# A third group of the first layer by seven products in its second matmul, and the second layer's first operands formed on GpSimd and read back from HBM

## The chip, the cores and the metric

One core of a Trainium2 chip runs the whole program. The metric is the time of one execution in device microseconds (us); the median of three runs is given for the kernel before. The engines are named as in the profile: PE (TensorE matmul), PEld (its weight load), DVE (VectorE), ACT (ScalarE), POOL (GpSimd) and SP (SyncE, which here only issues DMAs).

## What is computed

```python
x = attention(q, k, v, omega)                 # (4 batches, 8 heads, 576, 64) -> 2304 tokens x 512
x = square(maximum(x @ moe_w_in, 0)) @ moe_w_out        # first layer,  512 -> 2048 -> 512
h = x @ moe2_w_in                                       # second layer, 512 -> 2048 -> 512
g = where(h > 0, h, exp(minimum(h, 0)) - 1)
return g @ moe2_w_out                                   # float32, 2304 x 512
```

The attention is a linear one (random features, no softmax over tokens). All is float32. The change lies in the two layers alone.

## The kernel before

**Precision.** A float32 operand goes through PE as two limbs: a high one, cast on ACT to a rounded float32, and a low one, the rest, made on DVE by `minus` (L77). A product of two operands is three matmuls (high by high, high by low, low by high).

**Tiling.** Tokens come in four blocks of 512 (i = 0 to 3) and a left-over block B of 256. The hidden width of each layer is cut into four groups g of 512. A *tour* is one block in one group of one layer, written here (layer, group, block), so (0,3,1) is block 1 in the first layer's last group. Blocks go in the order 0, B, 1, 2, 3. The first group of the first layer is written apart; from (0,1,0) on a tour is one turn of the loop in `toured`.

**One tour.** The first product (`times`, L759) follows Strassen's scheme in Winograd's form: seven products of 12 matmuls (256 columns each) in the order b, t3, t2, p, t1, t4, q, named by the operand that is read; t1 to t4 are differences of quarters of x. In block B there are no seven products but four sets of 12. Behind the products stand additions on DVE (c22 at L1061, c21 at L1066), the activation on ACT, and the splitting into limbs. The second product of a tour runs between the first products of the *next* tour: `earlier(0)` to `earlier(3)` run four parts of it. In a group that is listed in `SECOND` these parts are again Winograd's seven products (`quadrants`, calling `strassen`, L836), 84 matmuls for a full block: p1 and p5, then p6 and p2, then p7 and p3, then p4. Their inputs are the four quarters of the activation (11, 12, 21, 22) and four differences t1 to t4 of them, made by `difference` (L924) and split by `halved` (L930, limbs at L77). In any other group of the first layer they are four calls of `chunk` (L818) of 24 matmuls, 96 in all, whose inputs are the four quarters alone. The left-over block has 48 either way. The sums of the outputs go into pages `ya` on DVE: `grown` (L910) for Strassen, `summed` (L942) for `chunk`.

**Chores.** Every tour also makes weights for a group to come: tiles are loaded by SP, an ACT and two DVE passes bring them into order (`cm` L135, `cv` L143 and L150), then they are cast (ACT, L189, `wh`) and their low limbs made (DVE, L77, `wl`). Where a weight's quarters are to be combined (all of w_in, and w_out of the groups in `SECOND`), each odd tile takes four more DVE operations of 128x256 (L171 to L174 for w_out, L176 to L179 for w_in). The chores are spread over the *slots* of the tour: `slot` stands four times in a full tour (between the products) and twice in block B.

**The second layer's operands.** When block i of the first layer's last group is done, `operands1` forms t1 to t4 from its four `ya` pages by `terms` on DVE at once (block B: one difference d), and puts seven splits (block B: three) into the list `later`. Each `slot` takes three of them: a cast on ACT (L621) and a `minus` on DVE. The limbs are written to HBM (`keep`, by SP) for the groups 1 to 3 of the second layer, which read them five products ahead (`read`, `XA = 5`). For group 0 of the second layer the limbs stay in SBUF: `split` enters them in `x_t`, and `read` skips that group.

**Order.** No scheduler moves anything: each engine executes in the order in which the program is written. An engine that waits holds up all that is written behind it on that engine.

## Time and profile before

| | |
|---|---|
| median of three runs | 911.29 us (911.05 to 911.65) |
| the profiled execution, its time | 911.45 us |
| its span in the trace | 909.7 us (1.75 us lie around it) |
| PE busy | 898.5 us, 99% |
| DVE busy | 682.3 us, 75% |
| ACT busy | 591.9 us, 65% |
| POOL busy | 86.7 us, 10%, all in the first 140 us |
| granted TensorE clock | full in all 40 slices of the span (the 2.4 GHz level) |

The first layer's group 2 (Strassen in both products) runs from 343.35 us, the start of tour (0,2,B), to 435.29 us, the start of (0,3,B), counted by its second products: 91.94 us. Group 3 (`chunk`) runs from there to 532.31 us: 97.02 us. Group 1 (Strassen) took 91.99 us, from 251.36 to 343.35. Tour starts that the text needs: (0,1,3) 302.32, (0,2,0) 322.98, (0,2,B) 343.35, (0,2,1) 360.07, (0,2,2) 375.65, (0,2,3) 395.54, (0,3,0) 415.42, (0,3,B) 435.29, (0,3,1) 452.29, (0,3,2) 468.47, (0,3,3) 489.74, (1,0,0) 511.05 us. Since PE is all but never idle, what matters in this profile is not a busy share but the few places where a PE row carries a bracket with an idle time, and the length of each tour against the number of its matmuls.

### The profile page before, as it was taken

Reading aid. Unit: us, or ns where it says so; the run is one execution under the profiler, and the core shown is the slowest. Engines: PE = TensorE matmul, PEld = TensorE weight load, DVE = VectorE, ACT = ScalarE, POOL = GpSimd, SP = SyncE. Lnnn points to the kernel's source line nnn. Section 1 sums busy time; section 2 is a strip of 40 time slices with the busy share of each in tenths; the row PEclk is TensorE's granted clock in tenths of the full one; section 3 lists DMA queues with packets and bytes.
Section 4 is the critical chain, followed back from the end, with each engine's and each line's share of the span. In section 5 each row is a group of like instructions: output and inputs, shape, how many; then the busy total and the mean of one; then the engine's idle time right before and its main releaser. Section 6 shows DMA issues by size and latency. Waiting matters only on the chain.

```text
span 909.7 us, 20185 instructions
## 1 busy us (share of the span) xinstructions
PE 898.5 (99%) x7637; PEld 839.5 (92%) x7637; DVE 682.3 (75%) x1254; ACT 591.9 (65%) x1260; POOL 86.7 (10%) x188
## 2 busy tenths in 40 slices
PE   8999999999999999999999999999999999999997
PEld 7888999998999999999999999899899889989986
DVE  5898874688786888777879897966597649766553
ACT  7999877664767675766266666755476638654551
POOL 4678730000000000000000000000000000000000
PEclk9999999999999999999999999999999999999999
DMA  9576522525998676577589654276458655662551
GB/s 249 160 196 159 170 83 80 172 93 173 330 375 300 210 253 236 178 234 254 192 290 333 237 207 162 93 255 203 166 196 272 226 165 191 231 206 92 214 179 70
DMA packets 132096, 183.84 MB, mean 202 GB/s; under 512 B 33952, under 2 KB 65696, under 8 KB 132000
## 3 DMA queue, kind: packets, MB, share of 16 engines
q1 hardware_dynamic: 131152, 182.14, 60.3%
q8 instruction: 60, 0.98, 0.4%
q10 hardware_dynamic: 848, 0.43, 0.2%
q14 instruction: 36, 0.29, 0.1%
HBM read 145.29 MB, written 37.22 MB: 201 GB/s over the span
## 4 chain that ended last, share of the span: by engine, by line
PE 88%; DVE 4%; ACT 4%; DMA 2%; issue 1%; SPq 0%; POOL 0%; DVEq 0%; ACTq 0%; POOLq 0%
PE py L810 22%; PE pb L759 13%; PE pa L759 8%; PE pw L759 8%; PE py L818 5%; PE ph L549 5%; PE py L585 5%; PE pb L836 4%; PE px L836 3%; PE po L759 2%; PE pe L759 2%; PE pr L836 2%; PE pn L437 1%; PE px L469 1%; DMA xsph<-xd00p 1%
## 5 line engine op out<-in xcount | busy, mean ns | idle before, releaser
L782 DVE SCALAR_TENSOR_TENSOR r<-r,t 128x512 f32<-128x512 f32 x72 | 49.5, 687 | 90.2 <-ACT t L781 90.2
L810 PE MATMUL py<-wh,gh 128*128 128x512 f32 x288 | 113.6, 395 | 0.0
L810 PE MATMUL py<-wl,gh 128*128 128x512 f32 x288 | 113.6, 394 | 0.0
L810 PE MATMUL py<-wh,gl 128*128 128x512 f32 x288 | 113.6, 394 | 0.0
L77 DVE TENSOR_TENSOR gl<-gf,gh 128x512 fp32r<-128x512 f32 (+1 forms) x122 | 77.3, 634 | 8.7 <-ACT gh L792 5.1
L810 PEld LDWEIGHTS py<-wh,gl 128*128 128x128 f32 x288 | 54.2, 188 | 12.7
L810 PEld LDWEIGHTS py<-wl,gh 128*128 128x128 f32 x288 | 54.2, 188 | 10.0
L810 PEld LDWEIGHTS py<-wh,gh 128*128 128x128 f32 x288 | 54.2, 188 | 9.9
L792 ACT CAST gh<-gf 128x512 fp32r<-128x512 f32 x72 | 44.4, 616 | 25.7 <-DVE gf L783 24.8
L942 DVE TENSOR_TENSOR ya<-py,ya 128x512 f32<-128x512 f32 x72 | 46.5, 683 | 7.0 <-PE py L810 6.1
L780 ACT ACTIVATE r<-gf 128x512 f32<-128x512 f32 x72 | 45.6, 633 | 2.3
L1047 ACT COPY pb<-pa 128x512 f32<-128x512 f32 x28 | 16.1, 574 | 46.1 <-PE pa L759 46.1
L135 ACT ACTIVATE cm<-st 128x512 f32<-128x512 f32 x64 | 44.3, 700 | 2.0 <-DMA st<-in_moe_w_out_dram 1.7
L1055 ACT COPY us<-pb 128x512 f32<-128x512 f32 x28 | 16.4, 586 | 43.4 <-PE pb L759 35.0
L781 ACT ACTIVATE t<-gf 128x512 f32<-128x512 f32 x72 | 44.3, 616 | 0.0
L150 DVE SCALAR_TENSOR_TENSOR cv<-cm,cv 128x512 uint32<-128x512 uint32 x64 | 43.3, 685 | 0.8
L1061 DVE TENSOR_TENSOR c<-pb,vs 128x512 f32<-128x512 f32 x28 | 19.3, 690 | 29.2 <-PE pb L759 23.4
L818 PE MATMUL py<-gh,wh 128*128 128x256 f32 x144 | 40.5, 282 | 0.0
L818 PE MATMUL py<-gh,wl 128*128 128x256 f32 x144 | 40.5, 281 | 0.0
L818 PE MATMUL py<-gl,wh 128*128 128x256 f32 x144 | 40.5, 281 | 0.0
L549 PE MATMUL ph<-xh,wh 128*128 128x256 f32 (+1 forms) x128 | 38.8, 303 | 0.0
L585 PE MATMUL py<-gh,wh 128*128 128x256 f32 (+1 forms) x128 | 38.5, 301 | 0.0
(1128 smaller groups left out, 3318.3 us busy)
## 6 DMA issues: line engine op xcount, KB each, us to landing
st<-in_moe_w_in_dram SPq DMA_DIRECT2D x32, 512.0 KB, 5.3
st<-in_moe_w_out_dram SPq DMA_DIRECT2D x32, 512.0 KB, 3.6
vk<-in_v_dram SPq DMA_DIRECT2D x32, 128.0 KB, 4.7
out_dram<-ya SPq DMA_DIRECT2D x16, 256.0 KB, 2.4
ld0k<-in_k_dram SPq DMA_DIRECT2D x4, 256.0 KB, 4.4
ld0q<-in_q_dram SPq DMA_DIRECT2D x4, 256.0 KB, 5.0
ld1k<-in_k_dram SPq DMA_DIRECT2D x4, 256.0 KB, 5.3
ld1q<-in_q_dram SPq DMA_DIRECT2D x4, 256.0 KB, 4.6
```

Of the source, the lines that this page charges most:

```text
L77: eng.tensor_tensor(out=out, in0=whole, in1=hi.bitcast(F32), op=ALU.subtract)
L135: nc.scalar.activation(out=staged[p][1], in_=staged[p][0][:, :, 1].bitcast(F32), func=AF.Prelu, scale=REBIAS, alpha=NEGATIVE)
L549: nc.tensor.matmul(ph[:, :n], wt[:, cs], x_part(xt, i, c)[:, n0:n1], start=(m == 0), stop=(m == 3 * KD - 1))
L585: nc.tensor.matmul(y, w[:, ts], a, start=j == 0 and m == 0 and t % per == 0, stop=j == GF - 1 and m == 2, skip_group_check=per > 1,)
L759: nc.tensor.matmul(y[:, pr * HN:(pr + 1) * HN], wt[:, ws], xs[v][:, e * HN:(e + 1) * HN], start=fresh and first and pr == 0 and m == 0, st ...
L780: nc.scalar.activation(out=r, in_=gf, func=AF.Exp, scale=-1.0)
L782: nc.vector.scalar_tensor_tensor(out=r, in0=r, scalar=1.0, in1=t, op0=ALU.add, op1=ALU.mult)
L792: nc.scalar.copy(out=gh, in_=gf)
L810: nc.tensor.matmul(y_t[l, u], a[:, s0], w, start=first and pr == 0 and m == 0, stop=last and pr == 1 and m == 2,)
L818: nc.tensor.matmul(y_t[l, u][:, e * HN:(e + 1) * HN], w[:, ts], a[:, pr * HN:(pr + 1) * HN], start=first and pr == 0 and m == 0 and e == 0 ...
L836: nc.tensor.matmul(y[:, e * HN:(e + 1) * HN], w[:, cs], a[:, pr * HN:(pr + 1) * HN], start=fresh and pr == 0 and e == 0 and m == 0, stop=p ...
L942: nc.vector.tensor_tensor(out=ya_t[key], in0=y_t[l, u], in1=ya_t[key], op=ALU.add)
```

## The change

Three things change, and with them the rows of the engines.

- `SECOND` gains (0,3): the first layer's last group makes its second product by seven products. Its w_out tiles then need the extra combinations.
- The second layer's operands: the four differences (block B: one) are formed by GpSimd instead of DVE, as entries of `later` among the splits, in the order b, t3 formed, t3, t1 and t2 formed, t2, p, t1, t4 formed, t4, q. Their limbs stay no longer in SBUF for group 0 of the second layer; that group reads them from HBM like the others, 31 pairs of 512 KB.
- The pace of `later` in the tours of the first layer's last group: two entries of a slot while block 0's or B's entries stand first, otherwise one, where it was three. Elsewhere it stays three.

```diff
-    SECOND = ((0,1),(0,2))
+    SECOND = ((0,1),(0,2),(0,3))
...
         kept.append(lambda: keep(moe, i, name, ((h,), (l,))))
-        if moe:
-            x_t[1, 0, i, name] = h, l
...
-    def terms(moe, i, b):
-
-        tt = nc.vector.tensor_tensor
...
-        tt(out=ts["t1"], in0=b[1, 0], in1=b[0, 0], op=ALU.subtract)
-        tt(out=ts["t2"], in0=b[1, 1], in1=ts["t1"], op=ALU.subtract)
-        tt(out=ts["t3"], in0=b[1, 1], in1=b[1, 0], op=ALU.subtract)
-        tt(out=ts["t4"], in0=b[0, 1], in1=ts["t2"], op=ALU.subtract)
...
-        made = [(name, b[l, k]) for name, l, k in PARTS[i == B]] + found
-        later.extend(lambda name=name, t=t: split(1, i, name, t) for name, t in made)
...
+            nc.gpsimd.tensor_tensor(out=ts[name], in0=ts.get(a, a) if isinstance(a, str) else a, in1=ts[c] if isinstance(c, str) else c, op=ALU.subtract)
...
+        made("b", (0, 0))
+        formed(("t3", (1, 1), (1, 0)))
+        made("t3")
+        formed(("t1", (1, 0), (0, 0)), ("t2", (1, 1), "t1"))
+        made("t2")
+        made("p", (0, 1))
+        made("t1")
+        formed(("t4", (0, 1), "t2"))
+        made("t4")
+        made("q", (1, 1))
...
-            if reads[n_read[0]][0][:2] != (1, 0):
-                load_x(*reads[n_read[0]])
+            load_x(*reads[n_read[0]])
...
-    def slot(chores, left):
+    def slot(tour, chores, left):
 
         run(kept)
         run(chores, -(-len(chores) // left))
-        run(later, 3)
+        n = 3 if tour[0] or tour[1] < NG - 1 else 2 if owed and owed[0] in (0, B) else 1
+        run(later, n)
+        del owed[:n]
```

In the order that the builds give, tile names carry layer, group and block, and a running number; L numbers are those of each kernel's own file (after: `strassen` L848, `grown` L922, `difference` L936, c22 L1075, c21 L1080).

DVE around the third slot of tour (0,2,2), where `cv0_12_1` and `cv0_13_1` are two w_out tiles of group 3 and `ya0` sums of the tour before. The kernel before:

```order
L910 TENSOR_TENSOR ya0_1_0_0_3525<-pr0_2_1_6494,ya0_1_0_0_3525 128x512
L910 TENSOR_TENSOR ya0_1_0_1_3527<-pr0_2_1_6494,ya0_1_0_1_3527 128x512
L910 TENSOR_TENSOR ya0_1_256_0_3711<-px0_2_1_6480,ya0_1_256_0_3711 128x512
L150 SCALAR_TENSOR_TENSOR cv0_12_1_6474<-cm0_12_1_6472,cv0_12_1_6474 128x512
L150 SCALAR_TENSOR_TENSOR cv0_13_1_6553<-cm0_13_1_6478,cv0_13_1_6553 128x512
L77 TENSOR_TENSOR gl22_0_2_2_6664<-g22_0_2_2_6630,gh22_0_2_2_6663 128x512
L910 TENSOR_TENSOR ya0_1_0_1_3527<-pb1_4651,ya0_1_0_1_3527 128x512
L910 TENSOR_TENSOR ya0_1_0_0_3525<-pb2_4653,ya0_1_0_0_3525 128x512
```

The kernel after:

```order
L922 TENSOR_TENSOR ya0_1_0_0_3525<-pr0_2_1_6494,ya0_1_0_0_3525 128x512
L922 TENSOR_TENSOR ya0_1_0_1_3527<-pr0_2_1_6494,ya0_1_0_1_3527 128x512
L922 TENSOR_TENSOR ya0_1_256_0_3711<-px0_2_1_6480,ya0_1_256_0_3711 128x512
L150 SCALAR_TENSOR_TENSOR cv0_12_1_6474<-cm0_12_1_6472,cv0_12_1_6474 128x512
L150 SCALAR_TENSOR_TENSOR cv0_13_1_6553<-cm0_13_1_6478,cv0_13_1_6553 128x512
L171 TENSOR_TENSOR cs0_13_1_6635<-cv0_13_1_6553 128x256
L172 TENSOR_TENSOR cv0_13_1_6553<-cv0_12_1_6474,cv0_13_1_6553 128x256
L173 TENSOR_TENSOR cs0_13_1_6635<-cv0_13_1_6553 128x256
L174 TENSOR_TENSOR cd0_13_1_6636<-cv0_12_1_6474,cs0_13_1_6635 128x256
L77 TENSOR_TENSOR gl22_0_2_2_6670<-g22_0_2_2_6630,gh22_0_2_2_6669 128x512
L922 TENSOR_TENSOR ya0_1_0_1_3527<-pb1_4651,ya0_1_0_1_3527 128x512
L922 TENSOR_TENSOR ya0_1_0_0_3525<-pb2_4653,ya0_1_0_0_3525 128x512
```

The four combinations of 128x256 now stand between the second L150 and `gl22`, the low limb of the quarter 22, as they do in group 1's tours for the tiles of group 2. The same stands in tour (0,2,3) for the tiles 14 and 15.

DVE from tour (0,3,1) into (0,3,2); `wl1_0b`, `cv1_3_0` and the four combinations are chores for the second layer, `gl` and `glt` are low limbs of this tour's activation. The kernel before:

```order
L77 TENSOR_TENSOR gl21_0_3_1_7759<-gf21_0_3_1_7730,gh21_0_3_1_7731 128x512
L77 TENSOR_TENSOR wl1_0b_7764<-cv1_1_0_7324,wh1_0b_7627 128x512
L150 SCALAR_TENSOR_TENSOR cv1_3_0_7696<-cm1_3_0_7629,cv1_3_0_7696 128x512
L176 TENSOR_TENSOR cs1_3_0_7767<-cv1_2_0_7537,cv1_3_0_7696 128x256
L177 TENSOR_TENSOR cv1_3_0_7696<-cv1_3_0_7696 128x256
L178 TENSOR_TENSOR cs1_3_0_7767<-cv1_3_0_7696,cv1_2_0_7537 128x256
L179 TENSOR_TENSOR cd1_1_0_7454<-cv1_2_0_7537,cs1_3_0_7767 128x256
L77 TENSOR_TENSOR wl1_0c_7772<-cs1_1_0_7453,wh1_0c_7631 128x512
L942 TENSOR_TENSOR ya0_4_0_0_4559<-py0_3_4_0_0_7553,ya0_4_0_0_4559 128x512
L942 TENSOR_TENSOR ya0_4_0_1_4561<-py0_3_4_0_1_7554,ya0_4_0_1_4561 128x512
L636 TENSOR_TENSOR d1_4_7776<-ya0_4_0_1_4561,ya0_4_0_0_4559 128x512
L77 TENSOR_TENSOR gl12_0_3_1_7818<-gf12_0_3_1_7754,gh12_0_3_1_7755 128x512
```

The kernel after:

```order
L936 TENSOR_TENSOR gt1_0_3_1_7750<-g11_0_3_1_7628,gt1_0_3_1_7750 128x512
L77 TENSOR_TENSOR wl1_0b_7761<-cv1_1_0_7347,wh1_0b_7634 128x512
L150 SCALAR_TENSOR_TENSOR cv1_3_0_7687<-cm1_3_0_7636,cv1_3_0_7687 128x512
L176 TENSOR_TENSOR cs1_3_0_7764<-cv1_2_0_7560,cv1_3_0_7687 128x256
L177 TENSOR_TENSOR cv1_3_0_7687<-cv1_3_0_7687 128x256
L178 TENSOR_TENSOR cs1_3_0_7764<-cv1_3_0_7687,cv1_2_0_7560 128x256
L179 TENSOR_TENSOR cd1_1_0_7496<-cv1_2_0_7560,cs1_3_0_7764 128x256
L77 TENSOR_TENSOR wl1_0c_7769<-cs1_1_0_7495,wh1_0c_7638 128x512
L77 TENSOR_TENSOR pl1_0_7772<-ya0_0_0_1_2970,ph1_0_7771 128x512
L77 TENSOR_TENSOR t1l1_0_7776<-t1_1_0_7644,t1h1_0_7775 128x512
L77 TENSOR_TENSOR glt2_0_3_1_7820<-gt1_0_3_1_7750,ght2_0_3_1_7819 128x512
L77 TENSOR_TENSOR gl12_0_3_1_7824<-g12_0_3_1_7746,gh12_0_3_1_7823 128x512
```

The two sums and the term of block B (`ya0_4`, `d1_4`) have gone from here; two low limbs of block 0's operands (`pl1_0`, `t1l1_0`) stand now ahead of `glt2` and `gl12`.

ACT in tour (0,3,1): `wh1_0b`, `cm1_3_0` and `wh1_0c` are chores, L621 the casts of block 0's operands, and the rows behind them the activation of the quarter 22. The kernel before:

```order
L189 CAST wh1_0b_7627<-cv1_1_0_7324 128x512
L135 ACTIVATE cm1_3_0_7629<-st1_3_0_7326 128x512
L189 CAST wh1_0c_7631<-cs1_1_0_7453 128x512
L621 CAST t3h1_0_7633<-t3_1_0_7489 128x512
L621 CAST t2h1_0_7637<-t2_1_0_7488 128x512
L621 CAST t1h1_0_7641<-t1_1_0_7487 128x512
L773 ACTIVATE r22_0_3_1_7681<-c220_3_1_7500 128x512
L774 ACTIVATE gh22_0_3_1_7683<-r22_0_3_1_7681 128x512
```

The kernel after:

```order
L189 CAST wh1_0b_7634<-cv1_1_0_7347 128x512
L135 ACTIVATE cm1_3_0_7636<-st1_3_0_7349 128x512
L189 CAST wh1_0c_7638<-cs1_1_0_7495 128x512
L621 CAST t3h1_0_7640<-t3_1_0_7568 128x512
L930 ACTIVATE g22_0_3_1_7681<-c220_3_1_7523 128x512
L931 ACTIVATE g22_0_3_1_7681<-g22_0_3_1_7681 128x512
L621 CAST t2h1_0_7694<-t2_1_0_7692 128x512
L930 ACTIVATE g21_0_3_1_7723<-c210_3_1_7522 128x512
```

One cast of an operand, that of t3, now stands ahead of the activation of 22 where three stood; the casts of t2 and t1 have moved behind it. In all, PE has 48 matmuls fewer, ACT 46 instructions more (1260 before), DVE 14 more (1254 before), POOL 17 more (128x512 each), and SP issues 62 reads of 256 KB more.

## Rows read from the trace of the kernel before

**Rows 1.** Page, part 1: busy us, share of the span, instructions.

```profile
PE 898.5 (99%) x7637; PEld 839.5 (92%) x7637; DVE 682.3 (75%) x1254; ACT 591.9 (65%) x1260; POOL 86.7 (10%) x188
```

**Rows 2.** Windows, one a tour; last five: us, engines busy (x), PEclk, DMA, GB/s.

```profile
302.32:322.98 20.66, 20.43 (x170) 20.03 (x169) 17.62 (x31) 14.04 (x27) 0.00 (x0) 1.00 0.78 254
322.98:343.35 20.37, 20.13 (x170) 19.93 (x169) 17.16 (x31) 14.73 (x27) 0.00 (x0) 1.00 0.70 234
343.35:360.07 16.72, 15.92 (x134) 15.72 (x133) 13.03 (x23) 9.44 (x18) 0.00 (x0) 1.00 0.70 236
360.07:375.65 15.58, 15.58 (x135) 15.58 (x134) 10.77 (x20) 8.54 (x15) 0.00 (x0) 1.00 0.57 187
...
395.54:415.42 19.88, 19.88 (x171) 19.88 (x169) 16.09 (x29) 13.99 (x26) 0.00 (x0) 1.00 0.83 280
415.42:435.29 19.87, 19.87 (x171) 19.87 (x169) 15.41 (x27) 12.94 (x25) 0.00 (x0) 1.00 0.68 217
452.29:468.47 16.18, 15.86 (x134) 15.65 (x133) 10.39 (x18) 9.75 (x18) 0.00 (x0) 1.00 0.66 227
489.74:511.05 21.31, 21.31 (x182) 21.31 (x181) 19.78 (x34) 12.34 (x22) 0.00 (x0) 1.00 0.84 299
```

**Rows 3.** Waits of PE, 234 to 640 us: releaser, idle us, count, largest.

```profile
PE px L836 <- DVE wl_10B L77: 0.8, 1, 0.8
...
PE pb L759 <- DVE c L1061: 0.3, 1, 0.3
```

**Rows 4.** Timeline of PE: start us, us, operation [idle before <-releaser].

```profile
307.43 0.39 PE L836 MATMUL pr<-glt,wh_4B 128*128 128x256 f32 x1 [0.23 <-DVE glt L77]
...
332.16 0.39 PE L836 MATMUL pb<-glt,wh_4C 128*128 128x256 f32 x1 [0.24 <-DVE glt L77]
...
347.99 0.39 PE L836 MATMUL px<-gh,wl_10B 128*128 128x256 f32 x1 [0.80 <-DVE wl_10B L77]
...
384.41 0.28 PE L836 MATMUL pb<-glt,wh_8C 128*128 128x256 f32 x1
...
466.95 0.39 PE L759 MATMUL pb<-xsqh,wh_12d 128*128 128x256 f32 x1 [0.32 <-DVE c L1061]
```

**Rows 5.** Timeline of DVE and ACT, tours (0,1,2) and (0,2,1).

```profile
301.79 0.42 DVE L171 TENSOR_TENSOR cs<-cv 128x256 f32<-128x256 f32 x1
...
370.26 0.69 DVE L1061 TENSOR_TENSOR c<-pb,vs 128x512 f32<-128x512 f32 x1 [2.61 <-PE pb L759]
...
371.03 0.60 ACT L189 CAST wh_12c<-cs 128x512 fp32r<-128x512 f32 x1
...
371.60 0.69 DVE L1066 TENSOR_TENSOR c<-pw,us 128x512 f32<-128x512 f32 x1 [0.65 <-PE pw L759]
...
374.56 0.69 DVE L77 TENSOR_TENSOR gl<-g,gh 128x512 fp32r<-128x512 f32 x1 [0.73 <-ACT gh L930]
...
377.65 0.69 DVE L77 TENSOR_TENSOR glt<-gt,ght 128x512 fp32r<-128x512 f32 x1 [0.48 <-ACT ght L930]
...
382.64 0.68 DVE L77 TENSOR_TENSOR glt<-gt,ght 128x512 fp32r<-128x512 f32 x1
```

**Rows 6.** Timeline of POOL and DVE in the attention stage.

```profile
118.48 1.04 POOL L321 TENSOR_TENSOR s23q<-ld3q 128x512 f32<-128x512 f32 x1
...
118.93 0.88 DVE L77 TENSOR_TENSOR gl<-gf,gh 128x256 fp32r<-128x256 f32 x1
...
113.28 0.44 DVE L77 TENSOR_TENSOR gl<-gf,gh 128x256 fp32r<-128x256 f32 x1
```

**Rows 7.** Windows: the stage from c22 of (0,3,1) on, and two stretches of DMA.

```profile
466.21:577.55 111.34, 111.02 (x846) 106.58 (x845) 98.82 (x170) 73.11 (x131) 0.00 (x0) 1.00 0.64 228
...
250.00:285.00 35.00, 35.00 (x297) 34.87 (x296) 26.03 (x45) 23.58 (x43) 0.00 (x0) 1.00 1.02 379
...
505.00:590.00 85.00, 85.00 (x600) 79.45 (x598) 75.61 (x128) 57.85 (x104) 0.00 (x0) 1.00 0.49 171
```

**Rows 8.** DMA issues: count, KB each, us to landing.

```profile
xst2h<-xd10t SPq DMA_DIRECT2D x3, 256.0 KB, 4.2
```

More of the change, by code (lines that the diff above doesn't have):

```diff
@@ L526, in linear_attention_two_ffn_kernel @@
     later, kept, unhurried, sums, carried, seeds = [], [], [], [], [], []
-    wholes = {}
+    wholes, owed = {}, []
     behind = [[], []]
@@ L629, in prepare @@
         run(later, n)
-    def terms(moe, i, b):
-        tt = nc.vector.tensor_tensor
-        if i == B:
-            d = page([W], f"d{moe}_{i}")
-            tt(out=d, in0=b[0, 1], in1=b[0, 0], op=ALU.subtract)
-            return [("d", d)]
-        ts = {name: page([W], f"{name}_{moe}_{i}") for name in TS}
-        tt(out=ts["t1"], in0=b[1, 0], in1=b[0, 0], op=ALU.subtract)
-        tt(out=ts["t2"], in0=b[1, 1], in1=ts["t1"], op=ALU.subtract)
-        tt(out=ts["t3"], in0=b[1, 1], in1=b[1, 0], op=ALU.subtract)
-        tt(out=ts["t4"], in0=b[0, 1], in1=ts["t2"], op=ALU.subtract)
-        return [(name, ts[name]) for name in ("t3", "t2", "t1", "t4")]
     PARTS = {False: (("b", 0, 0), ("p", 0, 1), ("q", 1, 1)), True: (("u", 0, 0), ("v", 0, 1))}
@@ L649, in operands1, with term, made, formed @@
         b = {(l, k): ya_t.pop((i, l, k)) for l in range(1 if i == B else 2) for k in range(2)}
-        found = terms(1, i, b)
-        made = [(name, b[l, k]) for name, l, k in PARTS[i == B]] + found
-        later.extend(lambda name=name, t=t: split(1, i, name, t) for name, t in made)
+        ts = {}
+        def term(name, a, c):
+            ts[name] = page([W], f"{name}_1_{i}")
+            a, c = (t if isinstance(t, str) else b[t] for t in (a, c))
+            nc.gpsimd.tensor_tensor(out=ts[name], in0=ts.get(a, a) if isinstance(a, str) else a, in1=ts[c] if isinstance(c, str) else c, op=ALU.subtract)
+        def made(name, key=None):
+            later.append(lambda: split(1, i, name, b[key] if key else ts[name]))
+            owed.append(i)
+        def formed(*terms_):
+            for t in terms_:
+                later.append(lambda t=t: term(*t))
+                owed.append(i)
+        if i == B:
+            made("u", (0, 0))
+            made("v", (0, 1))
+            formed(("d", (0, 1), (0, 0)))
+            made("d")
+            return
+        made("b", (0, 0))
[8 more added lines that the diff above has]
+        made("q", (1, 1))
     def piece0(d, i, l, k):
@@ L1004, in toured @@
                 chores = chores_of(tour)
-                slot(chores, 2)
+                slot(tour, chores, 2)
                 earlier(0)
@@ L1027, in toured @@
                     act_b(tour, "21")
-                slot(chores, 1)
+                slot(tour, chores, 1)
                 earlier(3)
@@ L1050, in toured @@
             chores = chores_of(tour)
-            slot(chores, 4)
+            slot(tour, chores, 4)
             earlier(0)
@@ L1057, in toured @@
             act(tour, "11", a)
-            slot(chores, 3)
+            slot(tour, chores, 3)
             earlier(1)
@@ L1068, in toured @@
             act(tour, "22", c22)
-            slot(chores, 2)
+            slot(tour, chores, 2)
             earlier(2)
@@ L1085, in toured @@
                 act_b(tour, "21")
-            slot(chores, 1)
+            slot(tour, chores, 1)
             earlier(3)
```

## The prediction

> **What bounds the kernel now.** I read the page first: PE is busy for 898.5 of 909.7 us, DVE for 682.3 [rows 1]. So a matmul less is time gained, as long as nobody makes PE wait instead. The second view is the length of each tour against its matmuls, by windows. A tour with 84 + 84 matmuls takes 19.88 us, so 0.1183 us for one; a tour of the last group with 84 + 96 takes 21.31 us, 0.1184 us for one [rows 2]. PE is at the 2.4 GHz level in every window (PEclk 1.00), so these lengths can be compared. The third view is PE's waits between 234 and 640 us: only a few, each below 1 us, and those of interest are on DVE [rows 3]. The fourth is the timeline around them. There one must not stop at the bracket: the tour from 302.32 us has 0.23 us in a bracket before `pr` [rows 4], yet it is 0.78 us longer than the tour from 395.54 us with the same matmuls [rows 2]; the matmul behind the wait is itself long (0.39 us). So I price a wait by the tour's length, not by its bracket. The last view is DVE's load where the change acts, from c22 of (0,3,1) on: 98.82 of 111.34 us, 170 instructions [rows 7]. That is the point of this case: PE gives up work there, and DVE gets more.
>
> **The change part by part.** All sums start from the profiled execution, 911.45 us (span 909.7 us and 1.75 us around it); the median of the three runs is 0.16 us lower.
>
> *Matmuls.* In four tours 96 become 84: 48 x 0.1184 = 5.7 us less. The block B tour keeps its 48.
>
> *One wait that goes.* The tour from 452.29 us is 16.18 us long; its 84 + 48 = 132 matmuls are worth 15.6 [rows 2]. PE waits there for c22 on DVE [rows 3, 4]. By the order of ACT three casts of operands stand before that point now, and one afterwards. I take the whole 0.6 us off.
>
> *Combinations of group 3's w_out.* Eight more DVE operations of 128x256, 0.42 us each [rows 5], come into tours (0,2,2) and (0,2,3), and three low limbs into the tours up to (0,3,B). The eight stand at the same places as in group 1's tours, whose order the changed tours repeat row by row. So I copy those lengths: the tour from 302.32 us takes 20.66 and that from 322.98 us 20.37, against 19.88 and 19.87 for group 2's without the combinations [rows 2]: 0.8 + 0.5 us. What is late there is `glt`, which PE needs for p5 and p6 [rows 4].
>
> *Block B of group 3.* With Strassen, (0,3,B) begins its second products with `w_out` combinations, as (0,2,B) does; there PE waits for `wl_10B` [rows 3, 4] and the tour takes 16.72 us, against 15.58 us for the same 132 matmuls in the next one [rows 2]. The new tour needs `wl_14B` at the same place: 1.1 us.
>
> *DVE and ACT between (0,3,1) and (0,3,2).* The nearest rows are those of (0,2,1), with the same products and no operands of the second layer. There c22 starts at 370.26 us, as soon as PE has its product (2.61 us of idle DVE before it) [rows 5]. In the changed kernel the cast of t3 stands behind the cast `wh..c` on ACT, which ends at 371.03 + 0.60 = 371.63 us [rows 5], and its low limb stands ahead of c22 on DVE: 371.63 + 0.60 + 0.69 = 372.92, so c22 is 2.7 us late. Behind it are three more low limbs (t2, p, t1) ahead of `glt2`: 3 x 0.69 = 2.1 us. Against these 4.8 us stand three idle gaps of DVE, 0.65 + 0.73 + 0.48 = 1.9 us, and the time from the end of the low limb `glt` (382.64 + 0.68 = 383.32 us) to the matmul that reads it (384.41 us), 1.1 us [rows 4, 5]. So PE waits 4.8 - 1.9 - 1.1 = 1.8 us at p6. The ends: nothing, if PE's own earlier delays make room, and 4.8 us.
>
> *The rest of the stage.* By the order DVE has seven operations more in the stage from 466.21 to 577.55 us (the three or four differences and sums of each Strassen tour, less the 17 terms). At 98.82 / 170 = 0.58 us each [rows 7] that is 4.1 us: 102.9 us in 111.34 - 5.7 + 2.1 = 107.8 us. DVE keeps 4.9 us of idle time, so it isn't the bound on the whole, only at places. For such a place in (0,3,3), where DVE is already busy for 19.78 us [rows 2] and the tour shrinks to about 19.9, I add 0.3 us (between none and 1). ACT, 73.11 us in this stage [rows 7], takes the 40 further instructions beside PE.
>
> *Terms on GpSimd.* An operation of 128x512 takes POOL 1.04 us. While it runs, a DVE operation that reads two SBUF tiles is held up: `gl` at 118.93 us takes 0.88 us, where the same at 113.28 us, with POOL idle, takes 0.44 [rows 6]. So each of the 17 terms costs DVE between nothing and 0.44 us. Seven of them fall into (0,3,1) to (0,3,3), where DVE has little room; I take a quarter of 0.44 for each, since many DVE operations there wait for PE or read PSUM: 0.8 us, with ends of 0 and 3.1.
>
> *Read back from HBM.* 31 pairs of 512 KB are 16.25 MB in some 85 us. That stretch moves 171 GB/s x 85 us = 14.5 MB now; it would be 362 GB/s. Between 250 and 285 us the kernel moves 379 GB/s with PE busy for all of its 35.00 us [rows 7]. A read lands 4.2 us after its issue [rows 8], and it is issued five products ahead, 5 x 12 x 0.118 = 7.1 us. I put it at nothing; without that cover PE would wait at the head of products.
>
> **Sum:** -5.7 - 0.6 + 0.8 + 0.5 + 1.1 + 1.8 + 0.3 + 0.8 = -1.0, so 910.45 us for the profiled execution and **910.3 us** on the scale of the median: of 6.3 us that leave PE's path, 5.3 come back as waits for DVE.
>
> **The rivals.**
>
> *The new waits don't come.* The copied ones (0.8, 0.5, 1.1) have rows, but 1.8, 0.3 and 0.8 are mine. If PE is late anyway by the earlier waits, DVE gains the room that I charge, and 911.45 - 6.3 + 2.4 = 907.6 us remain, 907.4 as a median; with none of the waits 905. For it: in (0,2,B) to (0,3,B) DVE has idle time enough to catch up within a tour. Against it: from 466 us on it hasn't.
>
> *GpSimd becomes what DVE waits for.* The mechanism is the row at 118.93 us, for each of the 17 terms: 17 x 0.44 = 7.5 us more on DVE in a stage where it keeps 4.9 us. If all of that idle time can be used, 2.6 us are left over, if none, 7.5; the middle is 5.0. With it in place of the 0.8: 910.45 - 0.8 + 5.0 = 914.7, some 914.5 as a median (912 to 917). It decides for slower from a mean delay of about 0.25 us a term: 17 x 0.25 = 4.2, less the half of the idle time, 2.4, makes up for the 1.8 us that the forecast without its 0.8 has in hand. For it: the row; against: it shows one short pair of operations, and POOL has nothing else to do in this stage. The Trainium skill, GPSIMD Engine Reference, section "8. Key points", says that GpSimd shares its SBUF interfaces with VectorE, in contention with DVE instructions that have two SBUF inputs or a 2-port mode; SBUF — State Buffer, section "SBUF: two separate sides", calls that pair of ports an exclusive lock for the whole instruction. By that rule a DVE operation could wait for up to a whole POOL operation, and the sum would gain up to 17 us rather than 7.5; the row at 118.93 us agrees with it in kind.
>
> *The read back is late.* If landing takes over 7.1 us, because SP's queue also carries the writes of the same limbs and the weights' loads, PE waits at the head of products. One us in each of four tours gives 4 us: 914.3 us. The rows speak against it by nearly 3 us a read.
>
> *Nothing comes of the change on PE's path* (the tours shrink by 12 matmuls and lengthen by waits at each of four places): 911.3 us.
>
> **How the numbers follow.** Forecast 0.48, with a range of its own from 908.5 to 912.2; new waits don't come 0.22 (905 to 908.5); GpSimd holds up DVE 0.16 (912 to 917); late reads 0.07 (913 to 915); nothing on the path, or a place that I don't see, 0.07. A difference of 0.2%, 1.8 us, is about what a measurement of this kernel can tell from no change: faster is below 909.5, slower above 913.1. Faster: 0.14 of the forecast and 0.22 = 0.36. Same: 0.32 of the forecast, 0.03 of GpSimd, 0.02 of the reads, 0.05 of the last case = 0.42. Slower: 0.02 + 0.13 + 0.05 + 0.02 = 0.22. The range from 906.3 to 914.0 leaves out the lower part of the second case (0.06) and the upper parts of the third and fourth (0.12).
>
> **What the changed profile would show.** Right: the second products of group 3 with 84 matmuls; the tours (0,2,3) and (0,3,0) at 20.7 and 20.4 us; (0,3,B) at 16.7 with a wait for `wl_14B`; PE waiting some 1.8 us in (0,3,2) for `glt2` at p6, and no wait for c22 in (0,3,1); DVE operations of 0.7 to 1.1 us beside POOL's 17. The second case shows as a group 3 of 92 us from (0,3,B) to (1,0,B) where it was 97; GpSimd's as many DVE rows over 0.69 us and a DVE without idle time from (0,3,1) on; the reads' as PE waits for `xs..1_0` tiles from DMA. The forecast is wrong if group 3 shrinks by over 4 us, or if any tour of the second layer's first group grows by more than half a us.

## The result and the profile after

The changed kernel takes 921.44 us (920.96 to 921.89, four runs) against 911.22 us; the ratio is 1.0116, 95% interval 1.0104 to 1.0128. The forecast was 910.3 us with a range up to 914.0: wrong in size and in sign. The loss is 10.2 us.

Part 1 of the page of the changed kernel, which answers to [rows 1]: the 48 matmuls are gone, and DVE is busy for 19 us more with 14 instructions more.

```profile
PE 899.8 (98%) x7589; PEld 836.9 (91%) x7589; DVE 701.3 (76%) x1268; ACT 615.4 (67%) x1306; POOL 115.5 (13%) x205
```

The windows of the changed kernel by tour, from (0,2,3) to (1,0,2), columns as in [rows 2], the engines in the order PE, PEld, DVE, ACT, POOL; the last row is the stretch from (0,3,2) to the end of (1,0,2).

```profile
394.85:415.52 20.67, 20.45 (x170) 20.09 (x169) 17.59 (x31) 14.04 (x27) 0.00 (x0) 1.00 0.79 260
415.52:435.95 20.43, 20.11 (x170) 19.90 (x169) 17.23 (x31) 14.74 (x27) 0.00 (x0) 1.00 0.69 229
435.95:452.61 16.66, 15.89 (x135) 15.68 (x134) 12.97 (x23) 9.44 (x18) 0.00 (x0) 1.00 0.64 217
452.61:468.24 15.63, 15.63 (x135) 15.63 (x134) 11.98 (x21) 8.98 (x16) 4.35 (x3) 1.00 0.37 120
468.24:490.89 22.65, 20.95 (x170) 20.13 (x169) 20.34 (x34) 18.05 (x35) 2.54 (x2) 1.00 0.93 315
490.89:512.37 21.48, 20.62 (x170) 20.01 (x169) 19.36 (x31) 17.15 (x32) 7.61 (x4) 1.00 0.97 348
512.37:537.86 25.49, 21.90 (x170) 21.08 (x169) 23.49 (x33) 16.88 (x32) 6.55 (x5) 0.96 0.92 316
537.86:555.20 17.34, 17.34 (x97) 15.25 (x97) 17.01 (x25) 10.61 (x19) 3.40 (x2) 0.96 0.76 251
555.20:571.14 15.94, 15.80 (x110) 14.38 (x108) 15.31 (x24) 10.94 (x20) 4.27 (x3) 1.00 0.77 247
571.14:596.06 24.92, 22.20 (x134) 19.15 (x133) 23.70 (x41) 20.81 (x38) 0.00 (x0) 1.00 1.04 388
468.24:596.06 127.82, 118.80 (x842) 110.00 (x841) 119.20 (x184) 94.43 (x173) 24.37 (x14) 0.99 0.91 318
```

The kernel before needs 117.29 us for the tours of the last row:

```profile
564.73:585.76 21.03, 21.03 (x134) 18.96 (x133) 20.36 (x36) 17.36 (x32) 0.00 (x0) 1.00 0.29 88
468.47:585.76 117.29, 117.29 (x878) 112.01 (x877) 104.56 (x179) 78.17 (x140) 0.00 (x0) 1.00 0.62 218
```

The first four tours are the copied ones, and they came as copied: 20.67, 20.43, 16.66 and 15.63 us, forecast 20.7, 20.4, 16.7 and 15.6. From (0,3,2) on the loss is 127.82 - 117.29 = 10.5 us, about all of the result. Two tours carry most of it: (1,0,0), 25.49 us where 19.9 were due (84 + 84 matmuls), and (1,0,2), 24.92 us where the kernel before takes 21.03. DVE is busy for 119.20 of 127.82 us, 14.6 us more than before, with five instructions more.

Where these 14.6 us come from is seen on the timeline of the changed kernel, DVE and POOL, at the terms (L639); here two of them with the DVE rows behind:

```profile
527.00 1.57 POOL L639 TENSOR_TENSOR t<-ya,ya 128x512 f32<-128x512 f32 x1 [6.07 <-PE pb L771]
527.34 1.78 DVE L77 TENSOR_TENSOR t1l<-t,t1h 128x512 fp32r<-128x512 f32 x1
...
529.64 0.68 DVE L1075 TENSOR_TENSOR c<-pb,vs 128x512 f32<-128x512 f32 x1
530.24 0.68 DVE L936 TENSOR_TENSOR g<-g,gt 128x512 f32<-128x512 f32 x1
...
531.05 1.31 POOL L639 TENSOR_TENSOR t<-ya,ya 128x512 f32<-128x512 f32 x1 [2.48 <-issue]
531.60 1.31 DVE L77 TENSOR_TENSOR glt<-g,ght 128x512 fp32r<-128x512 f32 x1 [0.69 <-ACT ght L942]
```

A low limb, 0.68 us alone, takes 1.31 to 1.78 us beside a term. Between 460 and 563 us thirteen DVE rows are stretched in this way, by 0.5 to 1.1 us each and 12.0 us in sum. A row that reads PSUM and one SBUF tile is not stretched, as `ya` at 470.22, wholly beside a term (c22 at 529.64 meets none):

```profile
470.19 1.29 POOL L639 TENSOR_TENSOR t<-ya,t 128x512 f32<-128x512 f32 x1 [5.76 <-DMA xd10t<-t3l]
...
470.22 0.68 DVE L922 TENSOR_TENSOR ya<-pr,ya 128x512 f32<-128x512 f32 x1
```

One term, at 500.66 us, took 4.70 us beside seven DVE rows without a gap, which kept their lengths; what held it is not shown.

What follows in (1,0,0) is a chain: `t1l` stands ahead of c22, c22 ahead of the difference t4 (530.24), and ACT and PE wait for that:

```profile
530.95 0.62 ACT L942 CAST ght<-g 128x512 fp32r<-128x512 f32 x1 [3.34 <-DVE g L936]
...
533.71 0.60 ACT L621 CAST qh<-ya 128x512 fp32r<-128x512 f32 x1
534.22 0.61 ACT L621 CAST bh<-ya 128x512 fp32r<-128x512 f32 x1
534.74 0.58 ACT L893 COPY pb<-pb 128x512 f32<-128x512 f32 x1
...
535.37 0.39 PE L848 MATMUL pb<-ght,wh_12A 128*128 128x256 f32 x1 [2.76 <-ACT pb L893]
...
535.94 0.41 PE L848 MATMUL pb<-ght,wh_12A 128*128 128x256 f32 x1
536.15 0.41 PE L848 MATMUL pb<-ght,wl_12A 128*128 128x256 f32 x1
```

ACT stands idle for 3.34 us, then does seven things, two splits of other blocks among them, before the copy that p4 needs; PE waits for 2.76 us. Behind the wait the matmuls start 0.21 us apart instead of 0.12: the granted clock has fallen (PEclk 0.96 in this window and the next), and 17 matmuls at the 1.2 GHz level cost another 17 x 0.095 = 1.6 us.

PE's waits of the changed kernel from 234 to 640 us, the answer to [rows 3] (releaser, us in total, times, longest):

```profile
PE pb L848 <- ACT pb L893: 2.8, 1, 2.8
PE pb L848 <- DVE glt L77: 2.2, 4, 1.2
PE pb L771 <- ACT pb L1061: 2.1, 2, 1.1
PE pw L771 <- DMA xst4h<-xd12t: 1.2, 1, 1.2
...
PE px L848 <- DVE wl_14B L77: 0.8, 1, 0.8
```

The wait for `xst4h`, a read from HBM, stands in (1,0,2), at 587.05 us. Two more there are for reads, `xsbl` at 571.72 (0.28 us) and `xst4l` at 587.69 (0.25): 1.7 us in all. A wait of 1.0 us for the copy `pb` (L1061) is in that tour too.

### The profile page after: what moved, and what is told of

Read it like the earlier page. It is cut to its first block, busy times and chain, and to the rows that moved or that the text cites. A ratio compares the mean times of both kernels' runs of the same rounds, so it can differ in the third digit from the quotient of the medians.

```text
span 920.1 us, 20331 instructions
## 1 busy us (share of the span) xinstructions
PE 899.8 (98%) x7589; PEld 836.9 (91%) x7589; DVE 701.3 (76%) x1268; ACT 615.4 (67%) x1306; POOL 115.5 (13%) x205
## 4 chain that ended last, share of the span: by engine, by line
PE 76%; DVE 10%; ACT 6%; DMA 5%; issue 2%; SPq 0%; POOL 0%; DVEq 0%; POOLq 0%; ACTq 0%
PE py L822 20%; PE pb L771 10%; PE pw L771 6%; PE pa L771 6%; PE ph L549 5%; PE pb L848 5%; PE py L585 5%; PE px L848 3%; PE po L771 2%; DVE ya L922 2%; PE pr L848 2%; PE pe L771 2%; PE pn L437 1%; DVE gt L936 1%; DMA xst4h<-xd03t 1%
## 5 line engine op out<-in xcount | busy, mean ns | idle before, releaser
L77 DVE TENSOR_TENSOR gl<-gf,gh 128x512 fp32r<-128x512 f32 (+1 forms) x104 | 68.3, 657 | 8.5 <-ACT gh L804 4.9
L639 POOL TENSOR_TENSOR t<-ya,ya 128x512 f32<-128x512 f32 x8 | 14.9, 1865 | 346.6 <-ACT bh L621 316.7
L150 DVE SCALAR_TENSOR_TENSOR cv<-cm,cv 128x512 uint32<-128x512 uint32 x64 | 45.5, 719 | 0.8
L1075 DVE TENSOR_TENSOR c<-pb,vs 128x512 f32<-128x512 f32 x28 | 19.3, 690 | 29.1 <-PE pb L771 22.2
L954 DVE TENSOR_TENSOR ya<-py,ya 128x512 f32<-128x512 f32 x54 | 34.8, 683 | 6.2 <-PE py L822 6.2
L585 PE MATMUL py<-gl,wh 128*128 128x256 f32 (+1 forms) x128 | 37.8, 295 | 0.0
L585 PE MATMUL py<-gh,wl 128*128 128x256 f32 (+1 forms) x128 | 37.8, 295 | 0.0
L549 PE MATMUL ph<-xh,wl 128*128 128x256 f32 (+1 forms) x128 | 37.7, 295 | 0.0
```

The costliest lines, as they stand in the source:

```text
L77: eng.tensor_tensor(out=out, in0=whole, in1=hi.bitcast(F32), op=ALU.subtract)
L150: nc.vector.scalar_tensor_tensor(out=t, in0=m.bitcast(U32), scalar=3, in1=t, op0=ALU.logical_shift_left, op1=ALU.bitwise_or)
L549: nc.tensor.matmul(ph[:, :n], wt[:, cs], x_part(xt, i, c)[:, n0:n1], start=(m == 0), stop=(m == 3 * KD - 1))
L585: nc.tensor.matmul(y, w[:, ts], a, start=j == 0 and m == 0 and t % per == 0, stop=j == GF - 1 and m == 2, skip_group_check=per > 1,)
```

## Experiments

All times are medians; a ratio is against the kernel before in the same job (910.6 to 910.8 us there), with its 95% interval. The changed kernel's own ratio is 1.0116.

| kernel | us | ratio |
|---|---|---|
| no_terms | 913.65 | 1.0032 (1.0020 to 1.0044) |
| dve_terms | 929.97 | 1.0211 (1.0196 to 1.0226) |
| resident | 925.07 | 1.0160 (1.0145 to 1.0175) |
| group3_only | 934.38 | 1.0249 (1.0231 to 1.0267) |
| no_group3 | 911.31 | 1.0006 (0.9997 to 1.0016) |
| readback_only | 910.23 | 0.9994 (0.9984 to 1.0003) |
| no_group3_pace3 | 910.36 | 0.9994 (0.9985 to 1.0004) |
| pace3 | 923.71 | 1.0141 (1.0124 to 1.0158) |
| pages89 | 932.22 | 1.0236 (1.0221 to 1.0251) |
| half_terms | 919.61 | 1.0097 (1.0081 to 1.0112) |
| no_lows | 910.43 | 0.9996 (0.9987 to 1.0006) |
| no_terms_lows | 907.71 | 0.9967 (0.9954 to 0.9980) |
| late_items | 921.76 | 1.0125 (1.0110 to 1.0140) |
| late_100 | 915.12 | 1.0046 (1.0029 to 1.0062) |
| late_100_n2 | 918.59 | 1.0088 (1.0071 to 1.0105) |
| late_half | 915.53 | 1.0052 (1.0037 to 1.0067) |
| late_half_n2 | 919.18 | 1.0092 (1.0077 to 1.0107) |

The theories at the start: (1) GpSimd holds up DVE; (2) the read back is late; (3) the seven products of group 3 overload ACT and DVE, whoever forms the terms.

### The parts alone

**group3_only** is the kernel before with one edit:

```diff
-    SECOND = ((0,1),(0,2))
+    SECOND = ((0,1),(0,2),(0,3))
```

> The kernel before with only the third group of seven products added (terms on DVE at once, limbs kept in SBUF, three splits a slot). Theory 3: tour (1,0,0) grows to 24 us or more here too, and the whole stays at 914 to 917 us. Theories 1 and 2: the extra time of the changed kernel comes from GpSimd and the read back, so this one shows what the matmuls give, 907 to 910 us.

It is the slowest of all. So a loss comes without GpSimd's terms and the read back too: with neither the third group loses 23.8 us, with both 10.2. Theory 3 has the direction right, but not the place: it is (0,3,2) and (0,3,3) that go wrong. Windows of the two tours:

```profile
469.01:500.72 31.71, 23.81 (x171) 22.48 (x170) 20.27 (x35) 19.18 (x35) 0.00 (x0) 0.92 0.86 314
500.72:530.12 29.40, 23.95 (x170) 23.44 (x169) 21.80 (x37) 17.33 (x32) 0.00 (x0) 0.85 0.59 206
```

PE and DVE both stand idle here for 5 to 11 us of a tour, at a granted clock of 0.85 to 0.92. A part of it is the clock: PE waits 3.85 us for one copy and then runs at half pace (the last two rows start 0.21 us apart, and 25 matmuls in a row so).

```profile
514.11 0.58 PE L836 MATMUL pb<-ght,wh_12C 128*128 128x256 f32 x1 [3.85 <-ACT pb L864]
514.49 0.41 PE L836 MATMUL pb<-ght,wl_12C 128*128 128x256 f32 x1
514.70 0.41 PE L836 MATMUL pb<-glt,wh_12C 128*128 128x256 f32 x1
```

**no_group3** (the changed kernel with `SECOND = ((0,1),(0,2))`):

> The changed kernel with group 3's second products left as they were before (four chunks of 24 matmuls); the terms on GpSimd, the read back and the pace stay. If these two cost time of their own, whatever the matmuls are: GpSimd's 17 terms some 7 us as between the changed kernel and the one without terms, and the late reads in block 2's tour 2 to 4 us, so 915 to 920 us. If they only cost something because group 3's seven products leave DVE no room (DVE is 89% busy in the stage before the change), they are nearly free here: 910 to 912.5 us.

**readback_only** (the kernel before without the two places that keep the limbs in SBUF):

```diff
-        if moe:
-            x_t[1, 0, i, name] = h, l
...
-            if reads[n_read[0]][0][:2] != (1, 0):
-                load_x(*reads[n_read[0]])
+            load_x(*reads[n_read[0]])
```

> The kernel before with the read back alone (terms on DVE at once, three splits a slot, two groups of seven products). If the reads themselves come too late when DMA carries 390 GB/s: waits for operands from DMA in the tours (1,0,0) to (1,0,3), 2 to 4 us, 913 to 915 us. If the late reads of the changed kernel are only the end of a chain that begins with late splits: no such waits and 910 to 911.5 us.

**no_group3_pace3** (no_group3 with `n = 3` in `slot`):

> The kernel before with the terms on GpSimd and the read back, but three entries a slot and two groups of seven products. Without the slow pace the stall of 2 us in (1,0,2) goes and the wait for c22 in (0,3,1) stays away if the terms let DVE pass: 909 to 910 us, at most 0.2% below the kernel before. If GpSimd's terms cost something of themselves: 911.5 us or more.

None of the three differs from the kernel before. Without group 3's seven products the terms on GpSimd, the read back of 16.25 MB and the pace are free: theory 2 is out as a cause by itself. One piece stays: no_group3 has (1,0,2) at 22.98 us where the kernel before has 21.03, no_group3_pace3 at 21.01; that is the slow pace, which leaves splits to that tour.

```profile
563.42:586.40 22.98, 21.34 (x134) 18.90 (x133) 22.21 (x39) 19.98 (x37) 0.00 (x0) 1.00 0.98 346
```

### Taken away from the changed kernel

**no_terms**:

```diff
-            ts[name] = page([W], f"{name}_1_{i}")
-            a, c = (t if isinstance(t, str) else b[t] for t in (a, c))
-            nc.gpsimd.tensor_tensor(out=ts[name], ...)
+            ts[name] = b[a]
```

> The changed kernel without its 17 terms: GpSimd forms nothing, and the splits that read t1 to t4 (or d) read a sum page in their place, so the second layer's input is wrong in those quarters; everything else is the changed kernel (921.4 us). Theory 1 (GpSimd holds up DVE): in the changed kernel's trace the 17 terms stretch a DVE operation of two SBUF inputs from 0.69 to 1.2 to 1.8 us, about 0.7 us each, 12 us in all, of which some 5 fall on tours where DVE is late: 916 us. Theory 2 (the read back is late, in block 2's tour of the second layer's first group, 3.9 us): that tour stays at about 24.9 us, total 920 to 921. Theory 3 (the seven products of group 3 in the second layer's first tour make ACT and DVE the bound there, whoever forms the terms): tour (1,0,0) stays above 24 us, total 919 to 921.

The terms are worth 1.0116 - 1.0032 = 0.0084, 7.7 us, more than the 5 that theory 1 gave them. (1,0,0) falls to 21.77 us, against theory 3, and (1,0,2) to 22.92, against theory 2. Yet 3 us of loss are left.

**dve_terms** (`nc.vector.tensor_tensor` in place of `nc.gpsimd.tensor_tensor` in `term`):

> The changed kernel with the 17 terms on DVE at the same places, in place of GpSimd. DVE gains 17 x 0.69 = 11.7 us of work and loses the hold-ups by GpSimd, some 12 us. Theory 1: no difference from the changed kernel beyond 1.5 us (920 to 923), but the long DVE rows of 1.2 to 1.8 us are gone. If GpSimd's share were free otherwise, so without a hold-up, DVE would be 11.7 us heavier and the time 925 or more. Theories 2 and 3 say nothing of this run but that their tours keep their lengths.

A miss of theory 1: some 9 us slower than the changed kernel, though DVE's 11.7 us of terms take the place of 12.0 us of hold-ups. The reason stands on the timelines of DVE and ACT in (0,3,2):

```profile
482.89 0.68 DVE L639 TENSOR_TENSOR t<-ya,t 128x512 f32<-128x512 f32 x1
...
483.66 0.62 ACT L621 CAST t4h<-t 128x512 fp32r<-128x512 f32 x1 [4.30 <-DVE t L639]
```

DVE is behind ACT here. A term on DVE comes when DVE gets there; ACT, whose cast reads it, stands for 4.30 us, and a copy that PE needs (`pb`, L876) stands right behind the cast. GpSimd, with nothing else to do, has its terms ready: from (0,3,2) to (1,0,2) of the changed kernel no wait of ACT over 0.3 us ends with a term. So it costs DVE as much time as it saves it, and still pays.

**resident** (the changed kernel with the limbs of the second layer's first group kept in SBUF):

> The changed kernel with the limbs for the second layer's first group kept in SBUF and not read back, as in the kernel before (62 reads of 256 KB less). Theory 2: tour (1,0,2) goes from 24.9 to about 21.0 us and no matmul waits for an operand from DMA in (1,0,0) to (1,0,3): 917 us, and less if the queue of SP also held up the writes. Theories 1 and 3: 920 to 921.5 us.

Against theory 2 on the whole: without the read back it is some 4 us *slower*. In its tour theory 2 is right in part: (1,0,2) falls from 24.92 to 22.94 us, and no matmul of it waits for a read any more. But (0,3,2) grows from 22.65 to 27.64 us. There ACT waits, in places where it doesn't in the changed kernel:

```profile
479.04 0.62 ACT L945 CAST gh<-g 128x512 fp32r<-128x512 f32 x1 [1.56 <-DVE t1l L77]
...
489.65 0.62 ACT L945 CAST ght<-g 128x512 fp32r<-128x512 f32 x1 [3.03 <-PE pb L851]
```

Neither releaser writes the tile that the cast reads; I read them as waits for the page that the cast writes. That pages are short there is argued from these rows alone.

**pages89** (`NPAGES = 89` in the changed kernel):

> The changed kernel with 89 pages of SBUF in its pool instead of 93. If free pages are what ACT and DVE wait for once group 3 has seven products (the kernel with the limbs kept in SBUF is 4 us slower, and its ACT casts wait for pages that DVE's splits release): 925 us or more. If pages are not short: 921 to 922 us.

The number came, but it does not show the reason. 9 us are lost ahead of (0,3,B), and from there to (1,0,3) both kernels take 160.11 us (444.90 to 605.01 here, 435.95 to 596.06 in the changed kernel). That is no sign that pages don't matter there, for the tours differ: (0,3,2) is 4.5 us longer than in the changed kernel, at a granted clock of 0.95, and (0,3,3), (1,0,0) and (1,0,2) are 0.7 to 1.5 us shorter each. That the sums agree is luck.

```profile
477.13:504.31 27.18, 22.17 (x170) 21.37 (x169) 22.35 (x37) 20.51 (x38) 2.65 (x2) 0.95 0.94 323
```

The changed kernel's own waits say more. Of those of ACT and DVE over 0.3 us from (0,3,2) to (1,0,2), one ends with something else than the writer of its input, so it looks like a wait for a page:

```profile
490.12 0.64 ACT L930 ACTIVATE g<-c 128x512 f32<-128x512 f32 x1 [1.54 <-DMA xd10t<-t4l]
```

So pages can stand behind a small part of the changed kernel's loss there; more is not shown.

**no_lows**:

```diff
         nc.scalar.copy(out=h, in_=t)
-        minus(nc.vector, l, t, h)
-        kept.append(lambda: keep(moe, i, name, ((h,), (l,))))
+        if not moe:
+            l = page([W], f"{name}l{moe}_{i}", F32R)
+            minus(nc.vector, l, t, h)
+        kept.append(lambda: keep(moe, i, name, ((h,), (h if moe else l,))))
```

> The changed kernel without the 31 low limbs of the second layer's operands on DVE (the high limb is written to HBM twice, so the second layer's first product has a wrong low part); the terms on GpSimd, the casts on ACT, the writes, the reads and the pace stay. Load theory: from (0,3,2) to (1,0,2) DVE is busy for 119 of 128 us in the changed kernel, and any 18 us of its work taken away there let the gain of group 3 appear: 907 to 912 us, below the kernel without terms. If it is GpSimd's hold on DVE at single places that costs the time, whatever DVE's load: 916 us or more.

**no_terms_lows** (both):

> The changed kernel without the 17 terms and without the 31 low limbs of the second layer's operands (the splits read a sum page in a term's place, and the high limb is written twice; the second layer's input is wrong). Load theory: without both, DVE has some 30 us less in the stage, and the whole gain of the 48 matmuls shows beside the waits of the weights' combinations: 906 to 908 us, and (1,0,0) at 19.9 to 20.5 us. If (1,0,0) is slow by the seven products themselves (eight ACT operations stand ahead of the copy that p4 reads): that tour stays at 21.7 us or more, the whole at 908.5 to 910 us.

Windows of (0,3,2), (0,3,3) and (1,0,0), first of no_lows, then of no_terms_lows:

```profile
467.98:487.83 19.85, 19.85 (x170) 19.85 (x169) 16.66 (x29) 18.32 (x35) 1.43 (x2) 1.00 1.00 368
487.83:507.69 19.86, 19.86 (x170) 19.86 (x169) 17.52 (x27) 15.51 (x29) 4.70 (x3) 1.00 1.05 392
507.69:530.74 23.05, 20.65 (x170) 20.04 (x169) 19.34 (x29) 16.79 (x32) 6.40 (x5) 1.00 0.88 314
```

```profile
467.92:487.80 19.88, 19.88 (x170) 19.88 (x169) 16.58 (x30) 18.75 (x35) 0.00 (x0) 1.00 1.01 365
487.80:507.69 19.89, 19.89 (x170) 19.89 (x169) 15.74 (x28) 14.89 (x29) 0.00 (x0) 1.00 1.04 382
507.69:528.03 20.34, 20.21 (x170) 20.00 (x169) 16.71 (x28) 17.06 (x32) 0.00 (x0) 1.00 0.99 351
```

In the four windows of 19.85 to 19.89 us DVE is busy for 15.7 to 17.5 us, and each tour is as long as its matmuls, with seven products, with DMA at 365 to 392 GB/s and with ACT busy for 14.9 to 18.8 us. So it is DVE's work for the second layer's operands, by its amount or by its place in the queue, that stands between the matmuls and their gain. (The terms and limbs left out also leave pages free, of which the changed kernel's waits show only the 1.54 us above; and the writes to HBM wait for no low limb, so that no matmul of (1,0,2) waits for a read.) Without both loads the kernel is 3.1 us below the kernel before. The forecast's matmuls, the wait that goes and the copied waits add up to 3.9, so they give about what they should. With the terms alone in place (no_lows) (1,0,0) is 2.7 us longer than without; there two terms fall on DVE rows on PE's path, `cv` at 506.88 us (1.78 us) and `glt` at 511.74 (1.72).

### Order and pace

**half_terms** (each term by two GpSimd operations of 128x256):

> The changed kernel with each of the 17 terms formed by two GpSimd operations of 128x256. If GpSimd holds DVE off for the whole of one operation, DVE gets in between the two halves: its long rows fall from 1.2 to 1.8 us to some 0.9 to 1.3, and the whole to 916 to 920 us. If the two engines share some port at half rate each, the delay is the same in sum: 921 to 922 us.

Some 1.7 us less than the changed kernel, and the intervals of the two ratios just overlap. The rows are clearer than the time. At the place of the rows of 527 us above, the timelines of POOL and DVE now read:

```profile
527.15 2.17 POOL L641 TENSOR_TENSOR t<-ya,ya 128x256 f32<-128x256 f32 x2 [5.43 <-PE pb L773]
...
527.49 1.22 DVE L77 TENSOR_TENSOR t1l<-t,t1h 128x512 fp32r<-128x512 f32 x1
528.64 1.22 DVE L77 TENSOR_TENSOR t4l<-t,t4h 128x512 fp32r<-128x512 f32 x1
```

DVE gets in between the two halves, so the hold-up is 0.5 us instead of 1.1, but it falls on two rows.

**pace3** (`n = 3` in `slot` of the changed kernel):

> The changed kernel with three entries of the list of splits and terms in every slot, as the kernel before has it, instead of one or two in the first layer's last group. If the slow pace pushes DVE work into the tours (1,0,1) and (1,0,2), where one stall of 2 us stands in the kernels without group 3 and without terms too: (1,0,2) returns to 21.1 us, and what group 3 loses by it decides; the load theory says that it only moves the time from there to (0,3,2) and (0,3,3), 920 to 925 us. If the pace is itself the cause: 917 us or less.

(1,0,2) returned to 21.01 us, and (0,3,2) grew to 25.5 us and (1,0,0) to 26.3: the time moves.

**late_items**: splits and terms are run behind `earlier` and behind c22 in the tours of the last group and of the second layer's first group:

```diff
             slot(tour, chores, 4)
             earlier(0)
             carry(0)
+            paced(tour)
...
             nc.vector.tensor_tensor(out=c22, in0=b, in1=vs, op=ALU.add)
             carry(1)
+            paced(tour)
...
             act(tour, "21", c21)
+            paced(tour)
...
             slot(tour, chores, 1)
             earlier(3)
+            paced(tour)
```

Here `paced` is the part of `slot` that takes entries of `later`.

> The changed kernel with the terms and splits of the second layer's operands written a step later in the tours of the first layer's last and the second layer's first group: behind the second products' part of a slot, and behind c22 or the activation, instead of ahead of them. If what PE waits for is late because these splits stand ahead of it on DVE and ACT (in (1,0,0) the low limb t1l, held up by GpSimd to 1.78 us, stands ahead of c22, and that ahead of the difference t4 that p4 needs): (1,0,0) falls from 25.5 to some 22 us and (0,3,2) by 1 us, the whole to 914 to 918 us. If DVE has too much work whatever the order: 920 us or more.

**late_100** (the later place in (1,0,0) alone, and the terms in halves):

> The changed kernel with two of the edits that helped a place: terms in two halves on GpSimd, and, in tour (1,0,0) alone, the terms and splits written a step later (behind c22, the activation and the parts of the second product). If the places add up: (1,0,0) at 21.8 us and the whole at 916 to 917 us. Load theory: what (1,0,0) gains comes back in (1,0,B) to (1,0,2), 918.5 to 920 us.

Windows of late_items, (1,0,0), (1,0,B) and (1,0,2), then of late_100, (1,0,0) and (1,0,2):

```profile
513.14:534.90 21.76, 20.24 (x170) 19.99 (x169) 19.77 (x29) 14.52 (x27) 6.12 (x4) 1.00 0.95 335
534.90:553.71 18.81, 17.31 (x99) 14.34 (x97) 18.55 (x28) 12.84 (x24) 3.33 (x2) 1.00 0.68 228
...
570.40:597.07 26.67, 23.80 (x132) 20.32 (x133) 23.95 (x42) 20.65 (x38) 0.00 (x0) 0.94 1.05 390
```

```profile
511.72:532.32 20.60, 20.06 (x170) 19.86 (x169) 18.66 (x31) 15.69 (x30) 7.33 (x8) 1.00 0.97 350
565.14:589.34 24.20, 22.14 (x134) 19.08 (x133) 23.42 (x41) 20.84 (x38) 0.00 (x0) 1.00 1.04 390
```

In late_items (1,0,0) gains 3.7 us and the next tours give it all back. In late_100 it gains 4.9 us, and of the second layer's tours only (1,0,2) stays long. The whole is 4.5 us below half_terms, which the load theory alone did not allow for. So a part of the loss is order: two casts and two low limbs of other blocks ahead of the one thing that PE waits for.

**late_100_n2** (late_100 with two entries a slot throughout the last group), **late_half** (late_100 with the later place in the last group too) and **late_half_n2** (both):

> The kernel late_100 (terms in halves, and splits and terms a step later in tour (1,0,0) alone; 915.1 us) with two entries of the list a slot throughout the first layer's last group, instead of one for the later blocks. If the tour (1,0,2), 24.2 us there and 21.0 in the kernel before, is long because the slow pace leaves too many splits to it: it falls to 22 us or less, and the whole to 912 to 914 us, unless (0,3,3) loses as much. Load theory: 914 to 916 us.

> The kernel late_100 with the later place for splits and terms in the tours of the first layer's last group too. If the order is what costs in (0,3,2) and (0,3,3), 22.5 and 21.1 us in late_100 against 19.9 when DVE is light: together 1 us less or more, 913 to 914.5 us. If DVE's load sets these two: 915 to 916 us.

> Both edits together: 911 to 914 us if they add up; 914 to 917 us if the time only moves.

The faster pace brings (1,0,2) to 22.20 us and (1,0,0) back up to 24.42; the later place gains 0.5 us in (0,3,2) and loses 1.3 in (0,3,3). No version with three groups and the whole computation reached the kernel before; late_100, at 1.0046, was the nearest.

## Why the prediction was wrong

**Right.** The matmuls (48, and 19.85 us tours where nothing waits). The wait for c22 in (0,3,1) went. The copied waits came within 0.06 us a tour, `wl_14B` included. The wait at p6 in (0,3,2) came as a wait for `glt`, 1.2 us in its bracket. By the tour's length, which is how the forecast prices waits, 1.8 us were forecast, and it is 2.8 us over its matmuls; in no_terms, at 22.08 us, it is 2.2 over them. The read back costs nothing where the second products of group 3 stay as they were (readback_only, no_group3_pace3).

**The step that failed is the term for GpSimd.** I took a quarter of 0.44 us for seven terms, 0.8 us; the terms cost 7.7. Three things in it were wrong. The row that I took the price from [rows 6] has a DVE operation of 128x256; the ones here are 128x512 and lose 0.5 to 1.1 us. (The row at 113.28 us that I set against it is not one with POOL idle, since a GpSimd operation from 112.17 us ends at 113.43; but 24 such rows that meet none take 0.43 us, so 0.44 stands as the price of that pair.) POOL's duration was that of an operation that reads one tile twice, 1.04 us; with two tiles it is 1.30, up to 1.77 beside DVE rows, and once 4.70. And most terms do meet such a row: 13 rows for 17 terms, 12.0 us, where even my upper end for all 17 was 7.5. Of the 7.7 us 3.7 are lost in (1,0,0) and 2.0 in (1,0,2), where the reads from HBM, which I had put at nothing, come late with the terms and not without. The rival "GpSimd becomes what DVE waits for" had the mechanism and the sign, with 914.5 us and a chance of 0.16; at the measured 0.7 us a term, its own working gives 17 x 0.7 = 12 instead of 7.5 us, 4.5 more, so some 919 us.

By the Trainium skill, GPSIMD Engine Reference, section "8. Key points", a DVE instruction with two SBUF inputs contends with GpSimd, and by SBUF — State Buffer, section "SBUF: two separate sides", whichever starts first keeps the shared ports for its whole instruction. The trace agrees: `t1l` at 527.34 ends at 529.12, 0.55 us behind the term's end at 528.57, which is nearly its own length of 0.68, and with halves the two engines take turns. It does not tell why the term at 500.66 us took 4.70 us. I had the rule beside the forecast and took the short row for the price.

**The second step is the idle time of DVE.** I counted 4.9 us of idle time in the stage as room, and three single waits. Without the terms the kernel is still 3 us above the kernel before, where my sum without its 0.8 has 1.8 below: 4.8 us more. Of these 1.9 us stand in (1,0,2), 22.92 us in no_terms: the pace, whose effect two tours later I had not costed (no_group3 shows it by itself). 1.9 us more stand in (1,0,0), 21.77 against 19.9, and 1.1 in (0,3,3), 21.26 against 20.2. These two go when DVE is light (no_terms_lows: 20.34 and 19.89). DVE, busy for about 90% of the stage, had no room at the places where its results are read; what counted was its load and the order of its queue at those places.

**What I hadn't thought of** is the clock as an amplifier: PE's wait of 2.76 us in (1,0,0) costs 1.6 us more behind it. And the read back, which I had as a risk, costs less than it saves: with the limbs kept in SBUF the changed kernel is slower by some 4 us, though the late reads of (1,0,2) are gone.

**Open.** How the loss in group3_only divides between pages, clock and order; how much of the loss left without the terms is DVE's load and how much its order; whether pages are what resident loses its time by; and what late_100 still loses in (0,3,2), (0,3,3) and (1,0,2), 22.50, 21.1 and 24.20 us.

## What to carry to other kernels

When an edit takes work from the bound engine, price what it adds to the engine next to it at the places where its results are read, not against its idle time on the whole stage: here 5.7 us of matmuls went, and some 16 came back, most of it behind waits for an engine that was 89% busy. An operation moved to GpSimd is not taken off DVE if DVE's neighbours read two SBUF tiles; it is paid for in longer DVE rows, and what it buys is that it is ready ahead of DVE's queue. Take the price of a collision from rows of the same size and the same number of inputs, or put the whole length of the other engine's operation into the range.
